# Score matmuls between the two transpose steps of a group in a top-k attention and mixture-of-experts kernel

## The chip, the cores and the metric

The kernel runs on one core of a Trainium2 chip. The metric is the device time of one execution in microseconds (us); lower is better. TensorE is called PE below, ScalarE ACT, VectorE DVE, GpSimd POOL, and SyncE, which issues most of the DMAs, SP.

## The reference

The input is `q`, `k`, `v` for 8 batches, 8 heads, 576 positions and 64 values a head, all float32. Each row of scores keeps its 32 largest values; the softmax runs over these alone. The attention's output, 4608 rows of 512 values, goes through a mixture of 8 experts, where each row takes one expert.

```python
scores = scale * np.matmul(q, k.transpose(0, 1, 3, 2))
kth = np.partition(scores, -top_k, axis=-1)[..., -top_k:-top_k + 1]
scores = np.where(scores >= kth, scores, -1000000000.0)
attn = np.exp(scores - np.max(scores, axis=-1, keepdims=True))
attn = attn / (np.sum(attn, axis=-1, keepdims=True) + 1e-09)
x = np.matmul(attn, v)              # then (B,H,S,D) -> (B*S, H*D)
expert_idx = np.argmax(x @ w_gate, axis=1)   # gate_w: its softmax weight
h = np.maximum(x_sorted[lo:hi] @ w1[e], 0.0)  # rows of expert e
y_sorted[lo:hi] = h @ w2[e]                   # out = gate_w * y
```

## The kernel before

**Units, tiles and groups.** Two heads make a unit; there are 8 batches of 4 units. The 576 queries of a head are four tiles of 128 and a tail of 64. A group is the same query tile of the unit's two heads, so that its scores are two blocks of 128 queries by 576 keys. Two units in a row give nine groups: tiles 0 to 3 of the first unit, one group of the tails of both units, and tiles 0 to 3 of the second. That makes 144 groups in the list `work`, and the main loop (`loop`, line 1175) takes one group in each turn. The turns are counted here from 0 to 143; "place" is a turn's number modulo 9, so that places 2 and 7 are the third tile (tile 2) of a unit, 3 and 8 its last tile, and 4 the tails.

**A group's way through the engines.** PE makes the scores (`products`, L299) in PSUM tiles `sc`. ACT copies them to SBUF (`scores`, L306, tile `s`). DVE finds the 32nd largest value of each row: it folds the 576 scores (L313 `h`, L315 `l`, L321 `few`, L323 `hl`, all of two SBUF inputs) and then takes eight maxima at a time (`search`, L361, L352, L369). ACT makes from the threshold a bound (L378 `low`) and a Relu that is zero for kept scores (L394), POOL subtracts it from the scores (`less`, L403), ACT takes the exponential (`weights`, L411). PE turns the weights: eight transposes of the first 512 keys (L422, PSUM tiles `wTm`), which ACT copies to `wT` (L429, for tails L427), and one or two of the last 64 keys of both heads (L438, for tails L436, PSUM tile `wTl`), which ACT copies to `wTt` (L446, L444). When a unit's last tile is through, PE multiplies with the values (L459 `po`), ACT copies (L461), PE turns the result (L470 `px`), and ACT copies again (L477).

**The order is written by hand.** The loop runs in a manual schedule for PE, ACT and DVE: each executes its instructions in the order in which the loop issues them. The groups overlap by software pipelining. In turn i DVE searches group i and folds group i+1; POOL and ACT make the weights of group i; ACT copies the scores of group i+3; PE transposes the weights of group i-1 and multiplies the scores of group i+4. `transposed` is a generator that the loop advances three times: the eight transposes and their two copies, then the `wTl` transpose, then the `wTt` copy.

**Blocks of the experts as filler.** The experts' matmuls are cut into pieces (`pieces`, L926 for the first weight matrix with PSUM tile `ph`, L943 for the second with `py`). A turn places some of its pieces between the two transpose steps (at most two, `part`), some after the second, and some at its end. How many is decided when the program is built, by a credit that the list of ready blocks fills. Pieces that are left when the loop is over follow it.

**Outputs in late steps.** A unit's last tile appends a generator `ending` to `late`. Its steps have names ("products", "relu", "rows" and others), and `at_place(name)` advances those that stand at that name. The matmuls of `outputs` are "products" steps.

**Buffers around the change.** `ps_s` holds the scores in PSUM and has two tiles, exactly one group. `ps_t` has two banks, for which `wTm`, `wTl`, `po` and `px` take turns: `wTl` waits until the first `wT` copy has emptied its bank. `load` has two `qkb` tiles, so the load of a unit's q and k on SP's queue waits until the scores of the last group of the unit two before are multiplied; `multiply` issues that load.

The order of a turn, with what does not touch the change left out:

```python
turns = turning(i - 1) if i else iter(())
next(turns, None)                              # eight transposes, two wT copies
part = min(BETWEEN, now - now // 2)
rest = pieces(part)
next(turns, None)                              # the wTl transpose
rest = pieces(now - now // 2 - part + rest)
weights(tiles, w_of[i], nbias)                 # ACT: two exponentials
next(turns, None)                              # ACT: the wTt copy
evacuate()
if i + AHEAD + 1 < len(work):
    multiply(i + AHEAD + 1)                    # scores of group i+4
```

Of the kernel before, what the change touches and what calls it, by code (L numbers as in the profile page):

```python
# [44 lines left out]
def kernel(  # L45
# [54 lines left out]
    NC = 4  # L100
# [148 lines left out]
    def groups(u):  # L249

        first, second = ([((a, i), (a, NC + i)) for i in range(NC)] for a in (u, u + 1))
        return first + [((u, 2 * NC), (u + 1, 2 * NC))] + second
# [49 lines left out]
    def scores(got):  # L302

        s = k.att.tile([P, 2, 2, HF], F32, name="s", bufs=2 if k.exact else 4)
        return s, [
            lambda m=m, ps=ps: nc.scalar.copy(s[:, m, :, :], ps[:, :, 0:HF]) for m, ps in enumerate(got)  # L306
        ]
# [527 lines left out]
    def evacuate(upto=None):  # L835

        while due and (upto is None or upto in [kind for kind, _ in due]):
            due.pop(0)[1]()
# [73 lines left out]
    def block(n, following=lambda: None, put_off=lambda store: store()):  # L912

        if not hasattr(n, "xT"):
            turned(n)
            yield "pause"
        evacuate("xT")
        hT = k.mlp.tile([P, FT, P], F32, name="hT", bufs=1)
        for half in range(2):
            while half and "y" in [kind for kind, _ in due]:  # L920
                yield "pause"
            ph = k.ps_m.tile([P, FT // 2, P], F32, name="ph", tag="m")
            for f in range(FT // 2):
                fc = half * (FT // 2) + f
                for dt in range(DT):
                    nc.tensor.matmul(  # L926
                        ph[:, f, :], n.w1[:, 0, dt, fc * P:(fc + 1) * P], n.xT[:, dt, :],
                        start=(dt == 0), stop=(dt == DT - 1),
                    )
                if f == FT // 2 - 1:  # L930
                    due.append((f"h{half}", lambda ph=ph, half=half: nc.scalar.activation(  # L931
                        hT[:, half * (FT // 2):(half + 1) * (FT // 2), :], ph, AF.Relu
                    )))
                yield
            if not half:
                finish()
        evacuate("h0")
        following()
        yield "pause"
        evacuate()  # L940
        py = bank("py") if k.apart else k.ps_m.tile([P, Dm], F32, name="py", tag="m")
        for f in range(FT):
            nc.tensor.matmul(py, hT[:, f, :], n.w2[:, 0, f, :], start=(f == 0), stop=(f == FT - 1))  # L943
            if f < FT - 1:
                yield
        y = k.mlp.tile([P, Dm], F32, name="y")

        def store():
            put_rows(n.x, y, P)

        def scaled():
            nc.scalar.activation(y, py, AF.Copy, scale=n.x[:, 0, Dm:Dm + 1])  # L952
            put_off(store)

        due.append(("y", scaled))
        yield "last"
# [8 lines left out]
    AHEAD = 3  # L965
# [4 lines left out]
    with fast:  # L970
# [7 lines left out]
        work = [(b, g) for b in range(B) for u in range(0, U, 2) for g in groups(u)]  # L978
# [15 lines left out]
        def landed(n):  # L994
            return clock is None or clock - n.at >= ON_CHIP
# [24 lines left out]
        def pieces(n):  # L1020
            nonlocal current, left
            while n > 0 and left > 0:
                if current is None:
                    if not landed(loaded[0]):
                        break
                    now = loaded.pop(0)
                    if hasattr(now, "half"):
                        current = long_block(now, following)
                    else:
                        current = block(now, following, stores.append)  # L1030
                    ahead()
                if clock is None:
                    evacuate()
                step = next(current)
                if step == "pause":
                    if clock is not None:
                        break
                    continue
                if step == "last":
                    current = None  # L1040
                n -= 1
                left -= 1
            return n
# [105 lines left out]
        late = []  # L1149
# [10 lines left out]
        def tiles_of(i):  # L1160
            b, g = work[i]
            return [(unit[b * U + u], tile) for u, tile in g]
# [4 lines left out]
        def multiply(i):  # L1167
            tiles = tiles_of(i)
            got_of[i] = products(tiles)
            n, tile = tiles[0]  # L1170
            more = n.b * U + n.u + 2
            if tile == (NC - 1 if n.u % 2 else 2 * NC) and more < len(units):
                unit.append(load_unit(*units[more]))

        def loop():
            nonlocal credit, rate, clock
            for i in range(min(AHEAD, len(work))):
                multiply(i)
                s_of[i], steps = scores(got_of.pop(i))
                for step in steps:  # L1180
                    step()
            multiply(AHEAD)
            f_of[0] = fold(s_of[0])
            fold_on(f_of[0])
            for i, (b, g) in enumerate(work):
                tiles = tiles_of(i)
                u, tile = g[0]
                if tile == 0 and u % 2 == 0:
                    open_unit(tiles[0][0])
                if tails(tiles):  # L1190
                    open_unit(tiles[1][0])

                then = lambda: None
                if i + 1 < len(work):
                    f_of[i + 1] = fold(s_of[i + 1])
                    then = lambda: fold_on(f_of[i + 1])
                low, nbias, doubts = search(tiles, s_of[i], f_of.pop(i), then)
                at_place("small")
                w_of[i] = depths(s_of[i], low)
                less(s_of.pop(i), w_of[i])  # L1200
                doubts()
                at_place("pool")
                at_place("relu")
                at_place("rows")
                put_stores()
                scatter(1)
                at = i % per_batch
                if at == FIRST and b:
                    rate = level(b) * PIECES / (U * NT)
                credit += rate * len(g)  # L1210
                room = left
                if b == B - 1 and at >= ARRIVED:
                    room -= KEEP
                    credit = room / (len(work) - i)
                share = {0: 0.5, 1: 1.2, 2: 1.6, 3: 0.5, 2 * NC: 1.4}[tile]
                now = max(0, min(int(credit * share + 0.5), room))
                credit -= now
                clock = i
                if i + AHEAD < len(work):
                    s_of[i + AHEAD], steps = scores(got_of.pop(i + AHEAD))  # L1220
                    for step in steps:
                        step()
                evacuate()
                at_place("turn")
                turns = turning(i - 1) if i else iter(())
                next(turns, None)
                part = min(BETWEEN, now - now // 2)
                rest = pieces(part)
                next(turns, None)
                rest = pieces(now - now // 2 - part + rest)  # L1230
                weights(tiles, w_of[i], nbias)
                next(turns, None)
                evacuate()
                if i + AHEAD + 1 < len(work):
                    multiply(i + AHEAD + 1)
                if tile == NC - 1:
                    end = ending(b, u)
                    late.append([end, next(end)])
                at_place("products")
                at_place("weights")  # L1240
                credit = min(credit + pieces(now // 2 + rest), 6 * rate)

            k.between = True
            for _ in turning(len(work) - 1):
                pieces(1)
            assert len(late) == 1
            clock = None
            for place in late[0][0]:
                if place == "rows":
                    pieces(4)  # L1250
            kept = left - (SURE + HALVES + PLAIN) * PIECES
            assert kept >= 0, kept
            k.apart = True
            pieces(kept)
# [20 lines left out]
    with ExitStack() as outer:  # L1275
        either = nc.values_load(rare_i[0:1, 0:1], min_val=0, max_val=P + 1)  # L1276
        outer.enter_context(tc.If(either > 0))
        with ExitStack() as st:
            open_pools(st, True)
            more = nc.values_load(rest_i[0:1, 0:1], min_val=0, max_val=LAST + E)  # L1280
# [5 lines left out]
        with ExitStack() as st:  # L1286
# [7 lines left out]
            with tc.For_i(0, B, 1) as b:  # L1294
# [3 lines left out]
                for u in range(0, U, 2):  # L1298
# [4 lines left out]
                    for g in groups(u):  # L1303
# [10 lines left out]
                        n, tile = tiles[0]  # L1314
# [76 lines left out]
```

## Time and profile before

| what | value |
|---|---|
| median of 3 runs | 1317.36 us (1315.74 to 1319.86) |
| the profiled execution's own time | 1319.47 us |
| its span from first to last instruction | 1317.9 us |
| PE busy (matmuls) | 1191.3 us, 90% |
| DVE busy | 1069.2 us, 81% |
| ACT busy | 931.7 us, 71% |
| POOL busy | 662.0 us, 50% |
| POOL `less`, L403 | 288 instructions, 1434 ns each |
| PE score matmuls, L299 | 1280 records, 463 ns each |
| DVE `few`, L321, over the first 1112 us | 144 instructions, 550 ns each |

The span has three stretches. In the first 500 us there are few pieces of the experts and PE has gaps. From about 500 to 1062 us the loop's turns are filled with pieces. After 1062 us DVE's searches are over and PE works off the remaining blocks. A busy share of the whole span mixes the three. The times of single instructions come from one profiled execution. Matmuls are pipelined, so the mean of one (463 ns) is longer than the step from one to the next: the eight records of a group's scores take 1.24 us together.

### The profile page before, as it was taken

Reading aid. Unit: us, or ns where it says so; the run is one execution under the profiler, and the core shown is the slowest. Engines: PE = TensorE matmul, PEld = TensorE weight load, DVE = VectorE, ACT = ScalarE, POOL = GpSimd, SP = SyncE. Lnnn points to the kernel's source line nnn. Section 1 sums busy time; section 2 is a strip of 40 time slices with the busy share of each in tenths; the row PEclk is TensorE's granted clock in tenths of the full one; section 3 lists DMA queues with packets and bytes.
Section 4 is the critical chain, followed back from the end, with each engine's and each line's share of the span. In section 5 each row is a group of like instructions: output and inputs, shape, how many; then the busy total and the mean of one; then the engine's idle time right before and its main releaser. Section 6 shows DMA issues by size and latency. Waiting matters only on the chain. (4 is left out here: it accounts for less than half of the span.)

```text
span 1317.9 us, 24504 instructions
## 1 busy us (share of the span) xinstructions
PE 1191.3 (90%) x7654; PEld 836.6 (63%) x7654; DVE 1069.2 (81%) x4617; ACT 931.7 (71%) x2136; POOL 662.0 (50%) x807
## 2 busy tenths in 40 slices
PE   5676777899889989999999999999999999999995
PEld 3343444655566556666666666667666777699973
DVE  8999999999999999999999999999999942000000
ACT  4788877888888887888788887898878851111110
POOL 2454546455755574658564745576558642000000
PEclk9788878999999999999999999999999999999998
DMA  4001013741473147434855554447454549986670
GB/s 149 29 30 30 30 38 102 267 161 39 137 265 140 46 156 282 174 110 148 299 173 182 166 210 173 165 150 292 145 204 149 205 154 311 378 284 212 212 291 18
DMA packets 98508, 220.94 MB, mean 168 GB/s; under 512 B 5181, under 2 KB 25917, under 8 KB 98368
## 3 DMA queue, kind: packets, MB, share of 16 engines
q1 hardware_dynamic: 91664, 199.02, 43.8%
q0 software_dynamic: 6416, 19.97, 4.2%
q8 instruction: 62, 1.02, 0.3%
q14 instruction: 78, 0.64, 0.2%
q10 hardware_dynamic: 288, 0.30, 0.1%
HBM read 195.88 MB, written 24.17 MB: 167 GB/s over the span
## 5 line engine op out<-in xcount | busy, mean ns | idle before, releaser
L403 POOL TENSOR_TENSOR w<-s,w 128x576 f32<-128x576 f32 x288 | 407.3, 1434 | 405.5 <-ACT w L394 405.4
L926 PE MATMUL ph<-xTs,w 128*128 128x128 f32 x2112 | 262.9, 279 | 5.1 <-ACT xTs L823 3.0
L926 PEld LDWEIGHTS ph<-xTs,w 128*128 128x128 f32 x2112 | 251.3, 194 | 24.3 <-issue 20.5
L943 PE MATMUL py<-w,hT 128*128 128x512 f32 x528 | 248.3, 599 | 3.9 <-ACT hT L931 3.7
L411 ACT ACTIVATE w<-w,nbias 128x576 f32<-128x576 f32 x288 | 224.1, 793 | 2.9 <-POOL w L403 2.2
L394 ACT ACTIVATE w<-s,low 128x576 f32<-128x576 f32 x288 | 207.6, 768 | 4.7
L299 PE MATMUL sc<-qkb 64*128 64x288 f32 (+1 forms) x1280 | 200.2, 463 | 9.4 <-ACT s L306 5.1
L422 PE MATMUL wTm<-turn,w 128*128 128x128 f32 x1152 | 166.9, 284 | 22.8 <-ACT xl L477 11.0
L422 PEld LDWEIGHTS wTm<-turn,w 128*128 128x128 f32 x1152 | 130.4, 144 | 79.7 <-issue 33.6
L306 ACT COPY s<-sc 128x576 f32<-128x576 f32 x288 | 168.7, 639 | 10.3 <-PE sc L299 10.3
L1270 DVE CAST any_i<-pd 1x1 int32<-1x1 f32 x1 | 0.1, 146 | 205.4 <-PE pd L1268 205.4
L361 DVE MAX8 tops<-scr 128x8 f32<-128x168 f32 x576 | 165.4, 315 | 0.0
L429 ACT COPY wT<-wTm 128x512 f32<-128x512 f32 x256 | 138.9, 603 | 23.8 <-PE wTm L422 23.7
L299 PEld LDWEIGHTS sc<-qkb 64*128 64x128 f32 (+1 forms) x1280 | 107.5, 191 | 70.0 <-issue 31.4
L361 DVE MAX8 tops<-few 128x8 f32<-128x144 f32 (+1 forms) x576 | 151.0, 300 | 0.0
L459 PE MATMUL po<-wT,vb 128*64 128x288 f32 x1024 | 150.0, 439 | 0.0
L943 PEld LDWEIGHTS py<-w,hT 128*128 128x128 f32 x528 | 91.9, 191 | 88.5 <-issue 82.6
L352 DVE MAX8 few<-l 128x8 f32<-128x288 f32 x288 | 127.1, 441 | 0.0
L841 POOL DMA_INDIRECT out_dram<-y,xg x37 | 38.9, 1052 | 173.5 <-ACT y L952 88.1
L459 PEld LDWEIGHTS po<-wT,vb 128*64 128x64 f32 x1024 | 72.5, 147 | 72.9 <-issue 21.6
L313 DVE TENSOR_TENSOR h<-s 128x576 f32<-128x576 f32 x144 | 109.3, 759 | 2.0 <-ACT s L306 2.0
L315 DVE TENSOR_TENSOR l<-s 128x576 f32<-128x576 f32 x144 | 108.6, 754 | 0.0
(188 smaller groups left out, 1654.5 us busy)
## 6 DMA issues: line engine op xcount, KB each, us to landing
w<-in_moe_w_dram SPq DMA_DIRECT2D x74, 2048.0 KB, 9.2
qkb<-in_qk_dram SPq DMA_DIRECT2D x31, 608.0 KB, 3.9
vb<-in_v_dram SPq DMA_DIRECT2D x32, 320.0 KB, 3.2
xg<-x_rows SPq DMA_DIRECT2D x37, 257.0 KB, 9.3
x_rows<-blank SPq DMA_DIRECT2D x13, 257.0 KB, 5.7
x_rows<-blank POOLq DMA_DIRECT2D x4, 257.0 KB, 9.7
x_rows<-x,posi POOLq DMA_INDIRECT x40, 3.5
out_dram<-y,xg POOLq DMA_INDIRECT x37, 4.1
```

Source lines behind the costliest of these rows:

```text
L299: nc.tensor.matmul(ps[rows, j, 0:HF], n.q[d, cols], n.k[d, keys], start=True, stop=True)
L306: lambda m=m, ps=ps: nc.scalar.copy(s[:, m, :, :], ps[:, :, 0:HF]) for m, ps in enumerate(got)
L352: nc.vector.max(out=f.few[:, m, QF + 8 * j:QF + 8 * j + 8], in_=away)
L361: nc.vector.max(out=tops[:, m, r * 8:(r + 1) * 8], in_=src[m])
L394: nc.scalar.activation(w[:, m, :], s[:, m, :, :].rearrange("p j k -> p (j k)"), AF.Relu, scale=-STEEP, bias=low[:, m:m + 1],)
L403: k.last_pool = in_turn(nc.gpsimd.tensor_tensor(w[:, m, :], s[:, m, :, :].rearrange("p j k -> p (j k)"), w[:, m, :], op=ALU.subtract)).ins
L411: nc.scalar.activation(w[:, m, :], w[:, m, :], AF.Exp, scale=scale, bias=nbias[:, m:m + 1], accum_out=n.z[:, c:c + 1])
L422: nc.tensor.transpose(pm[:, c * P:(c + 1) * P], w[:, m, first:first + P], ident)
L429: nc.scalar.copy(wT[:, :, m, q], pm4)
L459: nc.tensor.matmul(po[r, 0:HF], n.v[:, c, r], rhs, start=(c == 0), stop=(c == KC - 1))
L926: nc.tensor.matmul(ph[:, f, :], n.w1[:, 0, dt, fc * P:(fc + 1) * P], n.xT[:, dt, :], start=(dt == 0), stop=(dt == DT - 1),)
L943: nc.tensor.matmul(py, hT[:, f, :], n.w2[:, 0, f, :], start=(f == 0), stop=(f == FT - 1))
```

## The change

In turns whose tile is not a unit's last, and in which no late generator stands at "products", the scores of group i+4 are issued before the `wTl` transpose and the pieces behind it. In all other turns they stay where they were. The condition reads `late` in the middle of the turn, before the turn's own `at_place("products")`.

```diff
                 part = min(BETWEEN, now - now // 2)
                 rest = pieces(part)
+                more = i + AHEAD + 1 < len(work)
+                if more and tile != NC - 1 and not any(end[1] == "products" for end in late):
+                    multiply(i + AHEAD + 1)
+                    more = False
                 next(turns, None)
                 rest = pieces(now - now // 2 - part + rest)
                 weights(tiles, w_of[i], nbias)
                 next(turns, None)
                 evacuate()
-                if i + AHEAD + 1 < len(work):
+                if more:
                     multiply(i + AHEAD + 1)
```

## The prediction

> **What bounds the kernel now.** I read the page's first two parts, then the busy time by stretch, then each engine's waits, and last the order of time of PE and ACT around three moved turns.
>
> ```profile
> PE 1191.3 (90%) x7654; PEld 836.6 (63%) x7654; DVE 1069.2 (81%) x4617; ACT 931.7 (71%) x2136; POOL 662.0 (50%) x807
> PE   5676777899889989999999999999999999999995
> DVE  8999999999999999999999999999999942000000
> ```
>
> DVE is full until slice 32, PE from about slice 15 to the end. The stretches say it in us (span's stretch and length; busy time and instructions of PE, weight loads, DVE, ACT, POOL; granted clock; DMA):
>
> ```profile
> 18.00:512.00 494.00, 401.69 (x2547) 260.41 (x2548) 494.00 (x2157) 410.12 (x954) 284.28 (x353) 0.92 0.32 113
> 512.00:1062.00 550.00, 540.30 (x3653) 373.65 (x3652) 548.07 (x2320) 468.44 (x1085) 343.09 (x398) 1.00 0.53 183
> ```
>
> Until 512 us DVE sets the pace and PE idles 92 of 494 us: a wait of PE that is filled there is worth nothing. From 512 to 1062 us PE idles under 10 of 550 us. DVE looks as full, but part of that is stalls (below), so there the PE sets the pace and a wait that is added to it, or taken from it, moves the end. After 1062 us nothing is changed.
>
> The waits that the change is about (who waited for whom: us in total, times, longest):
>
> ```profile
> PE wTl L438 <- ACT wT L429: 61.9, 52, 3.9
> ACT wTt L446 <- PE wTl L438: 0.4, 1, 0.4
> ```
>
> PE waits often for the `wT` copy before `wTl`; ACT, in return, practically never waits for `wTl`. The change trades the one for the other. Turn 67 has such a wait (start, length, instruction, idle time before it):
>
> ```profile
> 500.39 0.60 PE L821 MATMUL xtp<-turn,xg 128*128 128x128 f32 x4
> 501.47 0.33 PE L438 MATMUL wTl<-turn,w 128*128 128x128 f32 x1 [0.47 <-ACT wT L429]
> 502.44 4.57 PE L926 MATMUL ph<-xTs,w 128*128 128x128 f32 x24 [0.65 <-ACT xTs L823]
> 506.94 1.24 PE L299 MATMUL sc<-qkb 64*128 64x288 f32 x8
> ```
>
> Turn 110 is the commoner kind from 512 us on; its pieces already cover the copy:
>
> ```profile
> 826.10 1.04 PE L422 MATMUL wTm<-turn,w 128*128 128x128 f32 x8
> 826.97 1.95 PE L926 MATMUL ph<-xTs,w 128*128 128x128 f32 x16
> 828.76 0.27 PE L438 MATMUL wTl<-turn,w 128*128 128x128 f32 x1
> 828.96 1.24 PE L299 MATMUL sc<-qkb 64*128 64x288 f32 x8
> 833.78 0.27 PE L438 MATMUL wTl<-turn,w 128*128 128x128 f32 x1
> ```
>
> ```profile
> 829.22 0.26 ACT L446 COPY wTt<-wTl 128x128 f32<-128x128 f32 x1
> 829.36 0.22 ACT L378 ACTIVATE low<-tops 128x2 f32<-128x2 f32 x1
> 832.65 1.07 ACT L429 COPY wT<-wTm 128x512 f32<-128x512 f32 x2
> ```
>
> PE goes from `ph` to `wTl` without a gap, ACT takes `wTl` 0.19 us after it is done (829.03 to 829.22), and behind that copy, without a gap, stand `low` and all of ACT's next turn.
>
> **What moves.** The built order of the changed kernel differs on PE in 41 of 143 turns: 2, 11, 20 and so on (place 2), 7, 16, 25 (place 7), nine tail turns (4, 13, 31, 49, 67, 85, 103, 121, 139) and turn 1. In each, four score matmuls (eight records) go ahead of `wTl`; no instruction is added. One step from `sc` to the next instruction is 1.17 us (828.96 to 830.13), so `wTl` and the pieces of its turn's middle come up to 1.17 us later, less what was a wait. What follows the old place of the scores starts when it did.
>
> **Edits at nothing.** The moved scores need the PSUM tiles that ACT's `s` copies empty; ACT does these before the `wT` copies (in turn 110 done at 825.2, the scores at 828.8), so no new wait; if that cover went, the loss is that of the row "sc waits for s", 5.1 us in four times. None of the moved groups is a unit's first, so none waits for a fresh `qkb`. Scores that come sooner let ACT's `s` copy start sooner, but that copy waited for PE only 10.3 us in six times, and where it did after 512 us, a `y` copy behind it waits for PE anyway. The moved step also issues a `qkb` load at place 4; SP's order changes at one spot, where this load goes ahead of one load of `w1`. SP then holds that `w1` load until the scores are done, which now come before the expert matmuls that stood ahead of them. I cost it at 0; at worst a PE wait like the one for weights at 1123.6 us, 2.1 us.
>
> **Turns before 512 us: 0.** ACT has finished early there and waits for DVE's threshold (`low` waits 66.1 us in 64 times). In turn 11, `wTl` waits 0.77 us; with the scores first it ends 0.40 us later, and ACT takes it only 1.5 us after its old end. With pieces ahead (turns 34 to 65) `wTt` is late by up to 0.93 us, but `low` behind it had 0.3 to 1.9 us of waiting in nearly all.
>
> **Gains from 500 us on: -2.3 us.** In turns 67 and 85 PE waits 0.47 + 0.65 and 0.48 + 0.65 us, for the `wT` and the `xTs` copy. The scores' 1.17 us fit into both: 1.12 + 1.13. All other moved turns after 512 us have no wait before `wTl`.
>
> **Losses from 512 us on: +5.3 us of PE waits.** In turns 70, 79, 88, 92, 97, 101, 106, 110, 115, 119, 124 and 128 ACT takes `wTl` 0.19 to 0.32 us after its end, so it loses 1.17 less that, 0.85 to 0.98 us. (Turns 83, 103, 121, 139 have 0.8 to 0.9 us in hand and lose 0.3 or less; 74, 133, 137 lose nothing.) The next turn is a unit's last tile, which isn't changed: PE's `wTl` stands behind at most one piece and needs ACT's `wT` copy. After turn 110 that copy ends at 833.24 and `wTl` starts at 833.78; 0.05 us is the signal, 0.49 in hand, so 0.93 late is 0.44 of new wait. The same reading gives 0.45 after 70, 79 and 92, 0.40 to 0.46 after 97, 101, 106 and 119; nothing after 88 and 124, where ACT stood idle for PE in between; 0.84 after 115, where nothing is in hand; and 0.96 after 128, where PE waits 1.11 us already (`wTl` at 966.82). Sum 3 x 0.45 + 0.40 + 0.44 + 0.42 + 0.44 + 0.46 + 0.84 + 0.96 = 5.3. Such a wait is not given back: the next ACT copies (`oT`, `wT`) wait for PE themselves. Net of the fills, +3.0 us.
>
> **POOL and DVE: +1.5 us, from -3 to +7.** `less` follows ACT's `low`, so in about ten of these next turns POOL's two L403 start 0.9 us later, and a DVE instruction with two inputs that meets one is held:
>
> ```profile
> 515.79 2.79 POOL L403 TENSOR_TENSOR w<-s,w 128x576 f32<-128x576 f32 x2 [6.71 <-ACT w L394]
> 517.40 1.50 DVE L321 TENSOR_TENSOR few<-h 128x288 f32<-128x288 f32 x1
> ```
>
> The same `few` took 0.45 us at 503.48, with POOL idle. The Trainium skill ("SBUF — State Buffer", section "SBUF: two separate sides") states that the port pair is locked for a whole instruction and the later one blocks fully. By that rule alone I estimate one L403 of 1.42 us for each of ten turns, 14 us, in place of the 1.5. Rows say less: at 532.59 `few` took 0.45 us although L403s ran on both sides of it. Where L403 began 2.7 to 4.3 us after the last threshold (turns 71, 80, 102, 107, 120, 125), 0.9 more brings it onto `few`, 5.7 us after; at 0.7 to 2.2 us each that is +7. Where it began later than 5 us (93, 111, 129) it may pass `few` and save 1 each, -3. But DVE isn't what ACT waits for in most of these turns (`low` starts 1 to 4.5 us behind the threshold), so a stall mostly uses up that lead; I take a fifth of the upper end, nearer the rows in which the lead is large.
>
> **Sum.** 3.0 + 1.5 = +4.5 us. The profiled execution took 1319.5 us (span 1317.9), 2.1 over the median of its runs; it would become 1324.0, and the median 1317.4 + 4.5 = 1321.9 us. That is 0.34%, close to the 0.3% (4.0 us) that a measurement of this kernel can tell from no change.
>
> **Rivals.**
> No difference: the terms are right, but the DVE term is zero, and the 0.79 us that PE waits at 1059.41 (turn 142, for `xl`, which follows DVE's last thresholds) swallows part: 3.0 - 0.8 = +2.2, 1319.6 us. For it: DVE's lead over ACT; against: DVE holds the last turns, where `low` waits for it again, so its delays do arrive. 0.37.
> Faster: the fill of turns 67 and 85 makes PE 1.1 us earlier at 512 us, where ACT begins to be late. If `low` comes less than about 1.7 us behind the threshold, L403 is over before `few`. In turns 69 to 107 the four folds are held for about 10 us; if half goes and the fills hold, -5 - 2.3 = -7, 1310 us. It decides if the lead of 1.1 us survives until turn 107; against it, the waits after 70, 79 and 92 eat 1.35 of it. 0.13.
> Not what it says: in 28 or so of the 41 turns the scores fill no wait that counts; that is part of the forecast.
> The forecast, slower by 4 us or more: 0.50. High end: losses 5.3 without the fills, and DVE +7: 1330. Low end: the faster case, cut at its nearer part, -5: 1312.
>
> **What would show it.** Right: the row "wTt waits for wTl" grows from 0.4 us to some 15 us in about 20 times; PE's idle time in 512 to 1062 us grows by about 3 us; `wTl` waits of about 0.5 us in turns 71, 80, 93, 98, 102, 107, 111; no wait before `wTl` in turns 67 and 85; DVE's thresholds unchanged until turn 66. Wrong: the end moves without those waits, `few` and `hl` are held much less than before, or PE idles less from 512 us on.

## The result, and the profile after

The changed kernel takes 1325.4 us (median of 6 runs, 1324.1 to 1327.1), against 1317.4 us for the kernel before in the same comparison: ratio 1.0062, 95% interval 1.0048 to 1.0076. That is slower by 8 us, 0.6%. The forecast was slower by 4.5 us (1321.9). The direction was right and the time lies in the range, but the sum is short by 3.5 us.

The first lines to compare are the page's busy times and its slices of PE and DVE:

```profile
PE 1198.9 (90%) x7654; PEld 838.6 (63%) x7654; DVE 1078.1 (81%) x4617; ACT 932.9 (70%) x2136; POOL 659.4 (50%) x807
...
PE   5776777899989989999999999999999999999995
...
DVE  8999999999999999999999999999999943000000
```

The shares and the slices are nearly the same as before. PE's busy time grew by 7.6 us and DVE's by 8.9, but the page doesn't say whether either costs anything. The busy time by stretch tells more (same columns as in the prediction):

```profile
18.00:512.00 494.00, 407.04 (x2534) 261.56 (x2535) 494.00 (x2143) 409.94 (x953) 283.86 (x351) 0.91 0.32 112
512.00:1062.00 550.00, 534.17 (x3590) 367.39 (x3588) 545.83 (x2279) 460.38 (x1065) 333.02 (x391) 1.00 0.51 181
```

From 512 to 1062 us PE now idles 550 - 534.2 = 15.8 us, where it idled 9.7 us before. What it waits for, and what ACT waits for, is in the engines' waits of the changed kernel in this stretch alone (us, times, longest):

```profile
ACT wTt L446 <- PE wTl L438: 12.6, 15, 1.1
...
PE wTl L438 <- ACT wT L429: 11.0, 20, 2.3
...
PE wTl L436 <- ACT wT L427: 2.4, 1, 2.4
```

Before, ACT's `wTt` never waited for `wTl` in this stretch, and PE's waits were shorter:

```profile
PE wTl L438 <- ACT wT L429: 5.2, 11, 1.1
PE wTl L436 <- ACT wT L427: 1.1, 1, 1.1
```

So the trade that the prediction described took place, ACT's new wait first and PE's one turn later. Over the whole span ACT's new wait is 17.3 us in 24 times, where the prediction named some 15 us in about 20. Turns 110 and 111 of the changed kernel, on PE and then on ACT, show it (start, length, instruction, idle time before it):

```profile
834.32 1.95 PE L926 MATMUL ph<-xTs,w 128*128 128x128 f32 x16
836.20 1.24 PE L299 MATMUL sc<-qkb 64*128 64x288 f32 x8
837.37 0.33 PE L438 MATMUL wTl<-turn,w 128*128 128x128 f32 x1
...
840.20 1.06 PE L926 MATMUL ph<-xTs,w 128*128 128x128 f32 x8
841.68 0.33 PE L438 MATMUL wTl<-turn,w 128*128 128x128 f32 x1 [0.42 <-ACT wT L429]
```

```profile
836.48 0.20 ACT L411 ACTIVATION_READ_ACCUMULATOR w<-w,nbias 128x1 f32 x1
837.74 0.27 ACT L446 COPY wTt<-wTl 128x128 f32<-128x128 f32 x1 [1.06 <-PE wTl L438]
837.90 0.21 ACT L378 ACTIVATE low<-tops 128x2 f32<-128x2 f32 x1
...
841.03 1.08 ACT L429 COPY wT<-wTm 128x512 f32<-128x512 f32 x2
```

ACT is done with the exponentials at 836.68 us and stands for 1.06 us until `wTl` is there. `low` and all of its next turn follow without a gap, the `wT` copies are as much later, and PE, which is through with its pieces, waits 0.42 us before the next `wTl`.

The fills came too. Turn 67 of the changed kernel has no wait:

```profile
504.71 0.60 PE L821 MATMUL xtp<-turn,xg 128*128 128x128 f32 x4
505.24 1.29 PE L299 MATMUL sc<-qkb 64*128 64x288 f32 x8
506.46 0.33 PE L438 MATMUL wTl<-turn,w 128*128 128x128 f32 x1
506.77 5.62 PE L926 MATMUL ph<-xTs,w 128*128 128x128 f32 x48
512.23 1.04 PE L422 MATMUL wTm<-turn,w 128*128 128x128 f32 x8
```

**Which trace to count against.** PE's delays in a turn are read here at the start of its eight transposes (`wTm`); "turn 144" is the last group's transposes, which follow the loop. Two differences between the traces of before and after are not the change's. The changed kernel's trace had lost 3.2 us already by turn 29, and it then won 3.9 us after the loop, because the trace of before has a wait for weights at 1123.62 us (2.08 us and a stretch of lower clock behind it) that the changed kernel doesn't meet. The two nearly cancel. To count the change by itself I use a trace with the old order from turn 66 on that shares both features, the kernel "early_only" of the first experiments: its PE stands 2.8 us behind the trace of before at turn 144, and its work after the loop takes 228.5 us, as in the changed kernel. Against it the changed kernel is 8.3 us later at turn 144, which agrees with the 8.0 us of the medians. That these two traces stand level where the loss begins is partly chance: the changed kernel's threshold of turn 66 comes 1.3 us sooner than early_only's, but in that turn its `sc` and `po` ran at a lower clock (1.85 and 3.19 us for 1.24 and 2.16), and at turn 67 its PE stands 0.13 us behind.

### The profile page after: what moved, and what is told of

Its sections match the earlier page's. It is cut to its first block, busy times and chain, and to the rows that moved or that the text cites. A ratio compares the mean times of both kernels' runs of the same rounds, so it can differ in the third digit from the quotient of the medians.

```text
span 1325.1 us, 24506 instructions
## 1 busy us (share of the span) xinstructions
PE 1198.9 (90%) x7654; PEld 838.6 (63%) x7654; DVE 1078.1 (81%) x4617; ACT 932.9 (70%) x2136; POOL 659.4 (50%) x807
## 5 line engine op out<-in xcount | busy, mean ns | idle before, releaser
L926 PE MATMUL ph<-xTs,w 128*128 128x128 f32 x2112 | 257.2, 275 | 0.0
L926 PEld LDWEIGHTS ph<-xTs,w 128*128 128x128 f32 x2112 | 248.4, 192 | 13.3 <-issue 12.8
L299 PE MATMUL sc<-qkb 64*128 64x288 f32 (+1 forms) x1280 | 205.9, 466 | 14.2 <-ACT s L306 9.9
L299 PEld LDWEIGHTS sc<-qkb 64*128 64x128 f32 (+1 forms) x1280 | 111.5, 191 | 76.8 <-issue 22.6
L459 PE MATMUL po<-wT,vb 128*64 128x288 f32 x1024 | 155.1, 451 | 0.0
```

The costliest lines, as they stand in the source:

```text
L299: nc.tensor.matmul(ps[rows, j, 0:HF], n.q[d, cols], n.k[d, keys], start=True, stop=True)
L459: nc.tensor.matmul(po[r, 0:HF], n.v[:, c, r], rhs, start=(c == 0), stop=(c == KC - 1))
L926: nc.tensor.matmul(ph[:, f, :], n.w1[:, 0, dt, fc * P:(fc + 1) * P], n.xT[:, dt, :], start=(dt == 0), stop=(dt == DT - 1),)
```

## The experiments

All times below are against the kernel before, run in the same comparison. Differences in us are the ratio's, taken of 1317 us.

### Which turns make the loss

Kernel early_only moves the scores in turns 0 to 65 alone, late_only in turns 66 and later alone:

```diff
-                if more and tile != NC - 1 and not any(...):
+                if more and i < 66 and tile != NC - 1 and not any(...):     # early_only
+                if more and i >= 66 and tile != NC - 1 and not any(...):    # late_only
```

> Only turns 0 to 65 have the scores moved; later turns are as before. Theory (the prediction's step: before 512 us PE's order costs nothing, and the 3.2 us that the changed kernel's trace has lost by turn 29 belong to that one execution): 1317.4 us, within 2 us, and no delay of DVE's thresholds against before at turn 66. Rival (the moved scores make the delay at turns 24 to 27, and DVE, which sets the pace there, hands it on): DVE's threshold of turn 66 some 3 us later than before, time 1318 to 1321 us, lower than 1317.4 + 3.2 only as far as the wait for weights at the tail takes it up (up to 4 us).

> Only turns 66 and later have the scores moved. Theory (the loss is PE's waits for wTl's successors and turn 103, all after 512 us, and the delay of turns 24 to 27 was no part of the change): about the changed kernel's 1325 us; with the delay of 3.2 us belonging to the early turns instead: about 1322 us. In both cases new waits before wTl of about 0.4 to 0.9 us in turns 71, 80, 93, 98, 102, 107, 111, 116, 120. Rival (DVE held by POOL, all over the loop, is the main loss): the waits are there, but the time is within 2 us of 1317.4.

Measured: early_only 1317.8 us, ratio 1.0003 (0.9991 to 1.0016); late_only 1325.2 us, ratio 1.0060 (1.0038 to 1.0083), +7.9 us. The whole loss is made from turn 66 on, and the moved scores of the first 66 turns cost nothing that can be seen. The delay of 3.2 us at turns 24 to 27 is no part of the change either: late_only has the old order there, and its thresholds are 3.05 us later than in the trace of before at turn 66. DVE's timeline of late_only shows where:

```profile
202.12 4.16 DVE L643 TENSOR_TENSOR past<-past,step_all 1x24 f32<-1x24 f32 x1
```

A small operation on one partition that took 0.15 us in the trace of before. So the expectation that early_only's threshold of turn 66 would match the trace of before was a miss: it came 4.4 us later. Since late_only, with the old order there, shows such a delay too, and since early_only's time is that of the kernel before, I count it as the scatter of executions (more at the end).

### Is it the late wTl?

Kernel copy_later keeps every moved score, but in turns of tile 2 ACT makes the `wTt` copy in the next turn, behind `low` and the Relus. Kernel between moves the same scores to behind `wTl` and ahead of the pieces that follow it.

```diff
                 weights(tiles, w_of[i], nbias)
-                next(turns, None)
+                if more or tile != 2:            # copy_later
+                    next(turns, None)
+                else:
+                    behind.append(turns)
...
                 less(s_of.pop(i), w_of[i])
+                while behind:
+                    next(behind.pop(), None)
```

```diff
                 rest = pieces(part)
+                next(turns, None)                # between: wTl first
                 more = i + AHEAD + 1 < len(work)
                 if more and tile != NC - 1 and not any(...):
                     multiply(i + AHEAD + 1)
                     more = False
-                next(turns, None)
                 rest = pieces(now - now // 2 - part + rest)
```

> All scores moved as in the changed kernel, but in turns of tile 2 ACT's copy of wTl (wTt) is issued in the next turn, behind low and the two Relus, so that ACT doesn't wait for the late wTl. Theory (ACT waits for wTl, is late with the next turn's wT copies, and PE waits for these before the next wTl): the row 'wTt waits for wTl' falls from 17 us to under 3, the new waits before wTl in the turns after tile 2 (71, 80, 93, 98, 102, 107, 111, 116, 120, 129; 5 to 6 us with what PE loses at each restart) are gone, time about 1319 us. The loss of turn 103, a tails turn, stays (2.9 us). Rival (the PE order itself, cold clock or DVE stalls make the loss): 1324 to 1326 us.

> The same turns have the scores moved, but to behind wTl instead of ahead of it: still ahead of the pieces behind wTl. In most turns of tile 2 nothing lies between, so their order is that of the kernel before; turns 67, 85, 103 and a few others differ. Theory: no late wTl, so no new wait of ACT for it, and no new waits before wTl; half of the fill of turns 67 and 85 stays (-1.3 us: the wait for the xTs copy), the loss of turn 103 stays in the main (up to +2.9 us, since the pieces behind the scores are what makes ACT late there): 1318 to 1320 us. Rival (the loss is not that of wTl's place): 1324 to 1326 us.

Measured: copy_later 1318.1 us, ratio 1.0000 (0.9989 to 1.0012); between 1317.9 us, ratio 1.0000 (0.9987 to 1.0013). Either way of sparing ACT the wait takes the loss away. In copy_later PE's order is the changed kernel's, so neither the order of PE's work nor the place of the scores costs anything by itself; what costs is ACT standing before `wTt`. Its waits from 512 to 1062 us:

```profile
PE wTl L438 <- ACT wT L429: 4.2, 10, 0.5
...
PE wTl L436 <- ACT wT L427: 2.4, 1, 2.4
...
ACT wTt L446 <- PE wTl L438: 1.0, 3, 0.4
```

PE's wait for `wT` is back to 4.2 us (in between to 5.6 us in 12 times, with one new wait, 0.34 us in turn 89, left), and turn 111 of copy_later has none:

```profile
838.56 1.06 PE L926 MATMUL ph<-xTs,w 128*128 128x128 f32 x8
839.45 0.27 PE L438 MATMUL wTl<-turn,w 128*128 128x128 f32 x1
```

From this pair and that of the changed kernel comes the price of such a wait. The step from `ph` to `wTl` is 0.89 us here (838.56 to 839.45) and 1.48 us with the wait (840.20 to 841.68): 0.59 us for a wait that is listed with 0.42 us. The records of these two matmuls overlap by 0.17 us in copy_later, and the wait takes that overlap as well.

The wait of 2.4 us at the tails' `wTl` (turn 104) stays in both kernels, as expected: it comes from turn 103, where the pieces behind the moved scores feed a Relu of ACT.

### The price of turn 103, and of the others

In turn 103 of the changed kernel 16 `ph` matmuls stand behind the moved scores and `wTl`, and end later. ACT's Relu of them (`hT`, L931) stands ahead of `low` of turn 104, on ACT's timeline:

```profile
780.66 0.60 ACT L931 ACTIVATE hT<-ph 128x512 f32<-128x512 f32 x1 [1.52 <-PE ph L926]
781.15 0.20 ACT L378 ACTIVATE low<-tops 128x2 f32<-128x2 f32 x1
```

Before, that wait was 0.70 us, and PE's in turn 104 was 1.09 us:

```profile
775.50 0.60 ACT L931 ACTIVATE hT<-ph 128x512 f32<-128x512 f32 x1 [0.70 <-PE ph L926]
780.05 0.41 PE L436 MATMUL wTl<-turn,w 128*64 128x128 f32 x2 [1.09 <-ACT wT L427]
```

PE's timeline, first of the changed kernel, then of late_only, which has the same order here:

```profile
785.21 0.43 PE L436 MATMUL wTl<-turn,w 128*64 128x128 f32 x2 [2.42 <-ACT wT L427]
785.57 2.29 PE L299 MATMUL sc<-qkb 64*128 64x288 f32 x8
787.79 2.68 PE L459 MATMUL po<-wT,vb 128*64 128x288 f32 x16
```

```profile
783.95 0.41 PE L436 MATMUL wTl<-turn,w 128*64 128x128 f32 x2 [2.42 <-ACT wT L427]
784.29 1.24 PE L299 MATMUL sc<-qkb 64*128 64x288 f32 x8
785.46 2.16 PE L459 MATMUL po<-wT,vb 128*64 128x288 f32 x16
```

The wait is 2.42 us in both, 1.3 more than before. Behind it the same matmuls took 4.97 us in one and 3.40 us in the other, 1.57 us apart. The granted clock (third number from the end) was 0.66 in the changed kernel and 1.00 in late_only:

```profile
785.00:790.00 5.00, 4.79 (x24) 2.60 (x26) 5.00 (x20) 4.31 (x11) 1.95 (x4) 0.66 0.57 235
785.00:790.00 5.00, 5.00 (x37) 2.86 (x34) 5.00 (x23) 4.93 (x13) 2.43 (x2) 1.00 0.41 151
```

So turn 103 cost 2.9 us in one execution and 1.3 us in the other. In copy_later's, where the clock behind this wait fell to 0.50, it cost 4.4 us. I first took the 2.9 for its fixed price, and tested it by leaving that turn out:

```diff
+                if more and i != 103 and tile != NC - 1 and not any(...):   # no_103
+                if more and tile == 2 and not any(...):                     # tile2_only
```

> All scores moved as in the changed kernel, but those of turn 103 stay behind. Theory (in turn 103 the ph pieces behind the moved scores make ACT's hT Relu late, which stands ahead of low(104); PE then waits 2.4 us in place of 1.1 us and runs the next scores and po at a lower clock): 2.9 us less than the changed kernel, 1322.5 us; PE's wait before wTl in turn 104 back at 1.1 us. Rival (the loss there would be given back by later waits): 1325 us.

> Only the turns of tile 2 (places 2 and 7) have the scores moved, not those of the tails. Theory: the new waits before wTl alone, about 8 us with their restarts; the fills of turns 67 and 85 (2.9 us with restarts) and the loss of turn 103 (2.9 us) are both gone and cancel: 1325 us. Rival (the waits overlap what turn 103 or DVE takes anyway): 1321 us or less.

Measured: no_103 1324.5 us, ratio 1.0064 (1.0049 to 1.0079), +8.4 us: no gain. The wait in turn 104 is back at 1.09 us as expected, and PE there was 1.3 us less late; but in this execution the clock dropped after another wait, at turn 129:

```profile
974.06 0.33 PE L438 MATMUL wTl<-turn,w 128*128 128x128 f32 x1 [2.28 <-ACT wT L429]
974.32 1.90 PE L299 MATMUL sc<-qkb 64*128 64x288 f32 x8
976.15 3.14 PE L459 MATMUL po<-wT,vb 128*64 128x288 f32 x16
```

In the changed kernel the same wait (2.29 us) was followed by 1.24 and 2.16 us. The expected gain of 2.9 us failed to come: what leaving out turn 103 saves by the traces, whatever the clock does, is 1.3 us, and the intervals can't tell that from nothing. tile2_only 1325.6 us, ratio 1.0080 (1.0060 to 1.0100): the turns of tile 2 alone make as large a loss. That fits the expectation that the fills of turns 67 and 85 and the loss of turn 103, all left out here, about cancel.

### The fills alone, and the waits added to them

Kernel two_turns moves the scores only where PE waits on both sides of `wTl`. Two kernels add to it: with_ten the ten turns of tile 2 whose next turns showed waits of 0.35 to 0.88 us, with_103_128 the two whose next turns showed 2.3 to 2.4 us. Kernel later_not_103 is copy_later without turn 103.

```diff
+                if more and i in (67, 85) and ...                                             # two_turns
+                if more and i in (67, 85, 70, 79, 88, 92, 97, 101, 106, 110, 115, 119) and ... # with_ten
+                if more and i in (67, 85, 103, 128) and ...                                   # with_103_128
+                if more and i != 103 and tile != NC - 1 and ...    # later_not_103, with the later copy
```

> Only turns 67 and 85 have the scores moved, where PE waits both before wTl and behind it. Theory: both waits are filled (1.12 + 1.13 us and a little for each restart), nothing is lost: -2.3 to -2.9 us against before, 1314.6 us. Rival (PE being earlier meets a wait for weights or for DVE later, which takes it back): 1317.2 us.

> As the kernel with the later wTt copy, but without the scores of turn 103 moved: all fills, no wait of ACT for the late wTl, no loss in turn 104. Theory: the later copy's 1318.1 us less 2.9 us: 1315.3 us, 2 us under before. Rival (the waits come back elsewhere, for DVE or for weights at the tail): 1317 to 1318 us.

> Turns 67 and 85 as in the kernel of two turns (1314.4 us), and besides the scores of ten turns of tile 2 moved (70, 79, 88, 92, 97, 101, 106, 110, 115, 119), each of which showed a new wait of 0.35 to 0.88 us before the next wTl. Theory (each such wait costs its length and some 0.2 us of restart: PE fell behind by 0.48 to 0.97 us at each, 6.7 us over ten): 1321 us. The prediction's step for the same ten turns (0.45 + 0.45 + 0 + 0.45 + 0.40 + 0.44 + 0.42 + 0.44 + 0.84 + 0.46 = 4.35): 1318.7 us. Rival (such waits are given back): 1315 us.

> Turns 67 and 85 as in the kernel of two turns (1314.4 us), and besides the scores of turns 103 and 128 moved, whose next turns showed waits of 2.4 us (in place of 1.1) and 2.3 us (in place of 1.1). Theory: the added idle time alone is 1.32 + 1.17 = 2.5 us, 1316.9 us, and each wait of over 2.2 us can be followed by a stretch of lower granted clock that costs some 1.6 us more, in some executions and not in others: up to 1320 us, the runs spread wider. By the prediction's steps (0.3 + 0.96): 1315.7 us.

| kernel | median us | before, same comparison | ratio (95%) | us |
|---|---|---|---|---|
| two_turns | 1314.4 | 1316.3 | 0.9986 (0.9975 to 0.9997) | -1.8 |
| later_not_103 | 1315.3 | 1316.3 | 0.9990 (0.9979 to 1.0002) | -1.3 |
| with_ten | 1322.2 | 1318.0 | 1.0026 (1.0012 to 1.0041) | +3.4 |
| with_103_128 | 1319.7 | 1318.0 | 1.0011 (0.9994 to 1.0028) | +1.4 |

The two fills alone make the kernel faster by 0.14%, an interval that just excludes no change, and two_turns is the version that beats both. With the later copy, moving all the other scores adds nothing that can be seen to that (later_not_103), and its distance from copy_later, in which turn 103 is moved too, is smaller than the intervals. The PE of two_turns idles less from 512 us on than that of before, by the busy time of that stretch:

```profile
512.00:1062.00 550.00, 541.19 (x3647) 373.31 (x3645) 545.43 (x2324) 470.58 (x1088) 343.52 (x402) 1.00 0.53 185
```

The parts add up. The ten waits cost 3.4 + 1.8 = 5.2 us over two_turns (about 2.8 to 7.7, the two intervals taken as independent; the traces put PE 6.4 us further behind from turn 68 to 121), the two long ones 1.4 + 1.8 = 3.2 us (about 0.6 to 5.9; traces 4.1 us). Fills, ten and two give -1.8 + 5.2 + 3.2 = +6.6 us, inside the 6.3 to 10.0 us of the changed kernel. Against two_turns the prediction's terms for the ten turns are 4.35 us and the traces' 6.4; the 5.2 us measured lie between, and the interval holds both. For the larger there are the traces alone, with_ten's being of the slowest of its twelve runs. With_103_128's medians rule out neither the idle time alone (2.5 us) nor the clock on top of it.

## Why the prediction was right, and where it was short

**Before 512 us: 0.** Right: early_only 1.0003. "DVE's thresholds unchanged until turn 66" failed as a sign, because thresholds move by 3 to 4 us from one execution to the next.

**Fills of turns 67 and 85, -2.3 us.** Right. The step from `xtp` to the next `wTm` in turn 67 is 7.52 us in the changed kernel against 8.88 us in early_only, -1.36; turn 85 gives -1.37, 2.7 us together; two_turns measures -1.8 (-3.3 to -0.4). The trace of before looks better for the fill than it is: its `ph` of 4.57 us there ran at a lower clock, where early_only's took 2.94 us.

**Waits of `wTl`, +5.3 us: right mechanism, mis-sized.** They came behind all ten turns named, with 0.55, 0.55, 0.54, 0.42, 0.51, 0.42, 0.42, 0.88, 0.47 and 1.18 us of added idle time for the 0.45, 0.45, 0.45, 0.40, 0.44, 0.42, 0.44, 0.84, 0.46 and 0.96 that were worked out. Turns 88 and 124, put at 0, made waits of 0.35 us (in turn 89) and 0.42 us (in turn 124 itself, at `py`, for `hT`). Together 6.7 us of idle time. The larger miss is that a wait was priced at its listed length. In these twelve turns the step from one turn's `wTm` to the next is longer than early_only's by 0.57 to 1.17 us, 8.9 us in all: 0.13 to 0.22 us more than each listed wait, save the last, where PE had waited before. The other turns give back 0.7 us in small amounts. The total agrees: by the traces, the changed kernel's PE is 1.5 us ahead of early_only's at turn 68 and 8.3 us behind at turn 144; that is 9.8 us lost, to which turn 85's gain of 1.4 us is added and from which turn 104's 2.9 us are taken, and 8.3 us are left for the `wTl` waits.

**"Turns 83, 103, 121, 139 lose 0.3 or less": failed for 103.** It looked at the `wTt` copy of that turn, which had time in hand, and not at ACT's Relu of the pieces behind it. The traces show 1.3 us of added idle time each time, and 1.6 us more by the clock in the changed kernel (none in late_only, 3.1 in copy_later). By times alone turn 103 was not told from nothing; together with turn 128 it was (with_103_128, +3.2 us over two_turns).

**POOL and DVE, +1.5 us: no part of the loss.** DVE's folds were held 5.5 us longer in all than in the trace of before (`hl` took 496 ns on average for 463, `few` 547 for 550), but PE's shift is accounted for by the waits above, and from 512 to 1062 us ACT waited less for DVE's thresholds than before (first before, then the changed kernel):

```profile
ACT low L378 <- DVE tops L361: 5.3, 9, 1.6
ACT low L378 <- DVE tops L361: 0.8, 3, 0.4
```

Copy_later and between don't separate this term, since in them ACT, and with it `less`, isn't late either. The estimate from the skill's page, 14 us, is further off.

**Rivals.** "No difference" counted on the 0.79 us before turn 142 to swallow part; that wait is still there, 0.86 us, since DVE's last thresholds moved with PE. "Faster" needed the lead of 1.1 us to live until turn 107; by turn 80 the new waits had eaten 0.7 us twice, as was said against it. "SP and `qkb`: 0" stands: late_only and the changed kernel have the same waits of `sc` for `qkb` as before within 0.2 us.

So the sum was -2.3 + 5.3 + 1.5 = 4.5 us; the traces say -1.5 - 1.4 + 8.3 + 2.9 = 8.3 us. The mechanism was right, but that the sum came as near as it did is in part luck: without the 1.5 us for DVE, which no run shows, it would have been 3.0 us.

## What to carry to other kernels

When an instruction is moved ahead of one that another in-order engine reads, look past the reader to everything behind it in that engine's queue, and past the pieces that the move pushes back to whoever reads those. Fill only the gaps that exist: two turns of the 41 had one that counted, and moving those alone gained 1.8 us where the rule for all lost 8. Count an added wait as the change of the step between two starts, not as the idle time that is listed, and count two profiled executions against each other only after finding where they differ in stretches that have the same order.

## What the runs showed of the hardware that I had not expected

**After waits of 2.3 to 2.4 us the granted clock dropped in some executions and not in others.** From 512 to 1062 us the changed kernel and its variants have ten waits of PE of 2.28 to 2.42 us. After six of them the granted clock of the next 5 us was between 0.50 and 0.67 (`sc` took up to 2.29 us for 1.24, `po` up to 3.98 for 2.16), after four it stayed at 1.00; the same wait in the same order went both ways. None of the twelve waits of 1.1 us that the traces have in this stretch was followed by a drop. That is no threshold: just before this stretch, where PE idles more often, a drop (0.66) followed the 1.72 us wait of turn 66 in the changed kernel, and none (1.00) followed the 1.68 us wait there in late_only. The Trainium skill ("TensorE: Matmul & The Clock Gate", "Part 1: The HAM clock gate") says that the array goes cold after at least one idle window of about 3.4 us; here drops came after shorter waits.

**One small DVE operation lasted as long as a whole train of POOL work.** The first of the eight L643 of an execution, 24 elements on one partition, took 4.15 to 4.17 us in ten of the twelve traces and 0.15 us in the two others (the kernel before and two_turns), where the operation ahead of it, L638, was held 1.37 us instead. In the changed kernel L643 starts at 202.65 us and ends at 206.8 us; POOL runs `lg`, `x` and two `less` back to back until 206.7 us:

```profile
202.54 0.26 POOL L501 TENSOR_TENSOR lg<-xl 128x40 f32<-128x40 f32 x1
202.77 1.25 POOL L509 TENSOR_TENSOR x<-xl,rz 128x640 f32<-128x640 f32 x1
203.98 2.75 POOL L403 TENSOR_TENSOR w<-s,w 128x576 f32<-128x576 f32 x2
```

In the trace of before POOL paused 1.41 us ahead of `less`, and L643 ran at once. Overlap and end times are what the traces show; that the shared port is the cause is the skill's rule that the prediction named, and was not tested by itself here. At turn 29 the ten traces stand 2.6 to 3.8 us behind that of before, and two_turns 0.2. The seven traces with scores moved before turn 66 are all among the ten, but so are three of the five with the old order there; early_only's time shows no cost of it.
